# Input product of a second MLP: eight groups of 11 block products per pass become five groups of 15 and one of 6

## The chip, the core and the metric

The program runs on one core of one Trainium2 chip. The metric is the device time of one execution in microseconds. The core has a matrix engine (TensorE, PE in the rows; its weight loads are PEld), VectorE (DVE), ScalarE (ACT), GpSimd (POOL) and SyncE (SP), which here only issues transfers. Each engine runs its own instructions strictly in their written order; they meet at semaphores.

## The reference

```python
x = attn_out.transpose(0, 2, 1, 3).reshape(3072, 384)          # from a linear-attention recurrence
a = x @ w_a;  b = x @ w_b                                      # 384 x 1536 each
x = (a * b) @ w_out                                            # first MLP, 1536 x 384
h = x @ w_in                                                   # second MLP, 384 x 2048: the product that changes
g = np.maximum(h, 0.0) + alpha * np.minimum(h, 0.0)            # alpha: one per column of h
out = g @ w_out2                                               # 2048 x 384
```

All in float32. The kernel takes each factor as a sum of a high and a low part and makes three matmuls (high*high, low*high, high*low) for one product.

## The kernel before, in words

**Stages.** The recurrence and the first MLP share the time up to about 586 us; the second MLP follows. It works transposed: features on the partitions, tokens in the columns. The 3072 tokens are six blocks of 512 and go through in three passes of two blocks (`mlp2(p, ...)`, p = 0, 1, 2). The 2048 hidden features are 16 groups of 128; the 384 inputs are 3 groups of 128, so a product of one feature group with one token block is 3 block products, and a matmul is 128x128 weights by 512 columns.

**Cells.** A cell is two feature groups by two token blocks, 12 block products by the plain rule. The kernel makes 11 (`cell`): sums of weight blocks (`load_c`, `sums` on GpSimd) are multiplied with sums of token blocks (`load_x2`, `comb` on GpSimd, `split` into high and low on ScalarE and VectorE), and the same partial sum serves several results. 11 products by 3 matmuls are 33 matmuls in a cell, 8 cells in a pass. A product or a chain of products runs in one of two PSUM banks (tag `h`, queue `psh`). After a product, a snapshot (`snap`, ScalarE) or an addition into an SBUF tile (`done`, VectorE) takes the bank's value; the bank's next matmul waits for that.

**Activation and output product.** A finished result (`tm`) goes through two Relu instructions on ScalarE, a VectorE instruction with alpha, a high part on ScalarE and a low part on VectorE (`g`). Nine matmuls a result and pass (`outs`) then add it to the six output banks (`oc`), one cell late; they are what TensorE does while a bank of `h` waits. At a pass's end VectorE transposes the six `oc` banks into tiles `O`, and SyncE (in the last pass ScalarE too) writes them out in packets of 128 bytes.

**Weights.** In pass 0 they are made from 64-bit inputs: a load issued by GpSimd, one ScalarE and one VectorE instruction that join the words (`load_w`), then high (ScalarE) and low (VectorE) of every tile; SyncE keeps the tiles in DRAM (`keeps`) and loads them again in passes 1 and 2 (`again`). Tiles live in 37 buffers of tag `w`, which the first MLP's 36 weight tiles hold until their last use.

**The order.** Nothing is ordered by hand. `add` records each step with an engine, an assumed duration, what it reads and writes and the buffer it needs; `Tasks.run` plans all of them with a list schedule, forward and backward eight times, and emits the instructions of the best plan. So every edit can move instructions everywhere.

Of the kernel before, what the change touches and what calls it, by code (L numbers as in the profile page):

```python
# [7 lines left out]
F32 = mybir.dt.float32  # L8
# [11 lines left out]
NT = B * S  # L20
# [347 lines left out]
def rwkv_then_moe_kernel(  # L368
# [721 lines left out]
    SL = {}  # L1090

    def load_x2(p, pr):

        raw, xs = {}, XS[p]
        for n in range(2):
            for kt in range(3):
                s = f"xr{n}{kt}"

                def ld(n=n, kt=kt, s=s):
                    at = 0  # L1100
                    for t, c0, cn in BLOCKS2[2 * p + n]:
# [28 lines left out]
        split("t2", "xr00")  # L1130
        comb("xr11", "xr11", "xr00", ALU.subtract)
        split("t1", "xr11")
        split("b32", "xr12")
        split("b21", "xr01")
        split("b31", "xr02")
        comb("xr01", "xr01", "xr00", ALU.subtract)
        split("t4", "xr01")

    def load_c(e, pr):

        ga = load_w(("i", 2 * e), wt2[2 * e, 0], pr, ["p2"])
        gb = load_w(("i", 2 * e + 1), wt2[2 * e + 1, 0], pr, ["p2"], fin=False)
        next(ga)
        yield
        next(gb)
        yield
        for g in (ga, gb):
# [12 lines left out]
        for i in range(4):  # L1160
            add(*SENG, pr, lambda i=i: sums(i), r=[r0, r1], w=[r1])
        for z, nm in ((1, "ws"), (0, "wc")):
            def hi(z=z, nm=nm):
                W[nm, e] = wp.tile([128, 2, 384], F32R, tag="w", name="w", bufs=NW)
                last = nc.scalar.activation(out=W[nm, e][:, 0], in_=RAW[r1][:, :, z].bitcast(F32), func=ACTF.Copy, scale=256.0).ins
                made["i", 2 * e + 1] = last

            def lo(z=z, nm=nm):
                nc.vector.scalar_tensor_tensor(
                    out=W[nm, e][:, 1], in0=RAW[r1][:, :, z].bitcast(F32), scalar=256.0, in1=W[nm, e][:, 0].bitcast(F32),  # L1170
                    op0=ALU.mult, op1=ALU.subtract)

            add("ACT", 0.455, pr, hi, r=[r1], w=[f"{nm}{e}"] + ([f"wi{2 * e + 1}"] if z == 0 else []), alloc=("w", f"{nm}{e}"))
            add("DVE", 0.46, pr, lo, r=[r1, f"{nm}{e}"], w=[f"{nm}{e}/l"])

    def keeps(e, pr):
        for k, nm in CELL(e, 0):
            add("SP", 0.6, pr, lambda k=k: nc.sync.dma_start(out=wsd[WI[k]], in_=W[k].bitcast(F32).rearrange("p z n -> p (z n)")),
                r=[nm, nm + "/l"], w=[f"kept{nm}"], nbytes=128 * 3072)

    def again(e, p, pr):
        for (k, nm), (k0, nm0) in zip(CELL(e, p), CELL(e, 0)):
            def ld(k=k, k0=k0):
                W[k] = wp.tile([128, 2, 384], F32R, tag="w", name="w", bufs=NW)
                nc.sync.dma_start(out=W[k].bitcast(F32).rearrange("p z n -> p (z n)"), in_=wsd[WI[k0]])

            add("SP", 0.6, pr, ld, r=[f"kept{nm0}"], w=[nm, nm + "/l"], alloc=("w", nm), nbytes=128 * 3072)

    def mlp2(p, pr):

        NE = F2 // 2
        xs, st, acc = XS[p], {}, {}

        def prod(ps, w, k, first, last, more):
            wt, at = w
            n = 0
            for wi, xi in ((0, 0), (1, 0), (0, 1)):
                nc.tensor.matmul(  # L1198
                    out=ps, lhsT=wt[:, wi, at:at + 128], rhs=SL[xs[k][xi]], start=first and n == 0, stop=last and n == 2, skip_group_check=more)
                n += 1  # L1200

        def cell(e, pr):
            par = (NE * p + e) % 2
            b = {}
            (kA, nA), (kB, nB), (kC, nC) = CELL(e, p)[:3]
            WA, WB, WC = (lambda k, x=x: (W[x], 128 * k) for x in (kA, kB, kC))

# [12 lines left out]
            tm = {o: f"TM{o}{par}" for o in range(4)}  # L1220

            def snap(bank, o):
                add("ACT", 0.58, pr - 20, lambda: nc.scalar.copy(SL[tm[o]], b[bank]), r=[f"h{bank}"], w=[tm[o]])  # L1223

            def done(bank, o, f, n):
                x, q, g = tm[o], f"TQ{o % NQ}", f"G{par}{o}"
                s = SL
                add("DVE", 0.69, pr - 20, lambda: tt(s[x], s[x], b[bank], ALU.add), r=[f"h{bank}", x], w=[x])
                if ACTP:
                    add("ACT", 0.62, pr - 20, lambda: nc.scalar.activation(out=s[q], in_=s[x], func=ACTF.Relu, scale=-1.0), r=[x], w=[q])  # L1230
                    add("ACT", 0.62, pr - 20, lambda: nc.scalar.activation(out=s[x], in_=s[x], func=ACTF.Relu), r=[x], w=[x])  # L1231
                    add("DVE", 0.69, pr - 20, lambda: nc.vector.scalar_tensor_tensor(  # L1232
# [329 lines left out]
```

## Time and profile before

| what | before |
|---|---|
| median of 3 runs (lowest, highest) | 979.55 us (977.29, 980.68) |
| the profiled execution | 978.45 us |
| its span, from the first to the last instruction | 976.6 us |
| TensorE busy | 953.7 us, 98% of the span |
| VectorE, ScalarE, GpSimd busy | 739.2, 528.5, 97.2 us |
| mean granted TensorE clock | 0.996 |

The span is 1.85 us shorter than the profiled execution's own time; the rest lies around the first and last instruction. Matmul ends are modelled, and about one matmul record in a hundred is missing, so distances between starts are safer than busy sums.

### The profile page before, as it was taken

The page shows a single profiled execution, that of the slowest core. Times are in us where ns is not written, and L with a number is a line of the kernel's source. Part 1 is how long each engine was busy: PE and PEld are TensorE (multiplying, and loading weights), DVE is VectorE, ACT ScalarE, POOL GpSimd, SP SyncE. Part 2 cuts the span into 40 slices and gives each one's busy share as a digit, 9 for nine tenths or more (in the row PEclk, how much of TensorE's full clock was granted, in tenths as well). Part 3 has the DMA queues.
Part 4 walks back from the last instruction along what each step waited for, and adds up shares of the span by engine and source line. Part 5 has one row for each costly group of instructions (what it writes and reads, how often), then busy time and mean ns, then how long its engine had stood idle before and what let it go on. Part 6 is the DMA issues. An engine that isn't in the chain of part 4 may idle for free.

```text
span 976.6 us, 20832 instructions
## 1 busy us (share of the span) xinstructions
PE 953.7 (98%) x8442; PEld 768.8 (79%) x8442; DVE 739.2 (76%) x1238; ACT 528.5 (54%) x1076; POOL 97.2 (10%) x157
## 2 busy tenths in 40 slices
PE   7999999999999999999999999999999999999996
PEld 4667887788788787888787887888888888888885
DVE  9989999798979998998935566865776455654544
ACT  0657563635444453453443567976766566665652
POOL 1112101000100000010015344110100000000000
PEclk9999999999999999999999999999999999999999
DMA  7797973404153341425025798515357344563203
GB/s 223 192 256 225 252 189 76 134 18 133 51 139 73 109 137 25 133 69 148 7 72 177 254 345 289 178 45 156 104 138 174 115 133 156 149 162 127 65 1 65
DMA packets 141199, 134.15 MB, mean 137 GB/s; under 512 B 101744, under 2 KB 112624, under 8 KB 139824
## 3 DMA queue, kind: packets, MB, share of 16 engines
q1 hardware_dynamic: 127408, 100.59, 36.7%
q0 software_dynamic: 7168, 31.45, 10.1%
q10 hardware_dynamic: 6528, 0.79, 0.5%
q8 instruction: 66, 1.08, 0.5%
q14 instruction: 29, 0.24, 0.1%
HBM read 104.68 MB, written 26.74 MB: 135 GB/s over the span
## 4 chain that ended last, share of the span: by engine, by line
PE 68%; DVE 21%; DMA 5%; issue 3%; ACT 1%; POOL 1%; SPq 0%; ACTq 0%; DVEq 0%; POOLq 0%
PE oc L966 19%; PE acc L966 8%; PE pb L966 8%; PE pa L966 8%; PE hx L1198 6%; PE hy L1198 5%; DVE Tp L414 4%; DVE e L414 4%; DVE A L633 3%; PE hu L1198 3%; PE hv L1198 3%; PE warm L1335 2%; PE psl L714 2%; DVE N L414 2%; DMA raw<-in_wt_dram 2%
## 5 line engine op out<-in xcount | busy, mean ns | idle before, releaser
L966 PE MATMUL acc<-g,w 128*128 128x512 f32 x648 | 173.8, 398 | 0.0
L966 PE MATMUL pb<-x,w 128*128 128x512 f32 x648 | 160.7, 392 | 2.8 <-DVE a L414 2.2
L966 PE MATMUL oc<-gx,w 128*128 128x512 f32 x648 | 162.8, 389 | 0.0
L966 PE MATMUL pa<-x,w 128*128 128x512 f32 x648 | 160.9, 393 | 0.9 <-ACT a L1023 0.9
L966 PEld LDWEIGHTS pb<-x,w 128*128 128x128 f32 x648 | 120.4, 188 | 29.9 <-DVE a L414 3.4
L966 PEld LDWEIGHTS pa<-x,w 128*128 128x128 f32 x648 | 121.2, 188 | 28.2 <-ACT a L1023 2.3
L966 PEld LDWEIGHTS oc<-gx,w 128*128 128x128 f32 x648 | 121.6, 188 | 25.3
L966 PEld LDWEIGHTS acc<-g,w 128*128 128x128 f32 x648 | 119.7, 189 | 24.9
L414 DVE TENSOR_TENSOR Tp<-Tp 112x1024 f32<-112x1024 f32 (+2 forms) x132 | 106.4, 806 | 1.2 <-DMA Tp<-in_rkw_t_dram 0.8
L1032 ACT CAST g<-a 128x512 fp32r<-128x512 f32 x72 | 44.6, 619 | 90.5 <-DVE a L414 74.5
L633 DVE TENSOR_REDUCE A<-e 128x16 f32<-128x768 f32 (+15 forms) x148 | 85.4, 577 | 0.9
L1023 ACT COPY a<-pa 128x512 f32<-128x512 f32 x72 | 42.1, 584 | 79.1 <-PE pa L966 68.0
L1223 ACT COPY tm<-hx 128x512 f32<-128x512 f32 x72 | 42.3, 588 | 77.9 <-PE hx L1198 77.3
L1198 PE MATMUL hx<-xs,w 128*128 128x512 f32 x288 | 80.9, 389 | 0.0
L1232 DVE SCALAR_TENSOR_TENSOR tm<-tm,al 128x512 f32<-128x512 f32 x96 | 72.7, 760 | 5.2 <-ACT tm L1231 5.1
L1230 ACT ACTIVATE tm<-tm 128x512 f32<-128x512 f32 x96 | 60.1, 627 | 24.5 <-DVE tm L414 24.0
L414 DVE TENSOR_TENSOR tm<-tm,hy 128x512 f32<-128x512 f32 x24 | 16.5, 688 | 73.1 <-PE hy L1198 73.1
L414 DVE TENSOR_TENSOR g<-a,g 128x512 fp32r<-128x512 f32 x72 | 49.4, 687 | 27.1 <-ACT g L1032 27.1
L414 DVE TENSOR_TENSOR a<-a,pb 128x512 f32<-128x512 f32 x72 | 48.9, 680 | 27.3 <-PE pb L966 23.0
L1198 PEld LDWEIGHTS hx<-xs,w 128*128 128x128 f32 x288 | 54.1, 188 | 11.3
L1231 ACT ACTIVATE tm<-tm 128x512 f32<-128x512 f32 x96 | 59.9, 625 | 1.4
L453 ACT ACTIVATE ws<-raw 128x384 f16<-128x384 bf16 x68 | 42.8, 642 | 31.3 <-DVE raw L459 15.3
(94 smaller groups left out, 1345.5 us busy)
## 6 DMA issues: line engine op xcount, KB each, us to landing
w<-wsd SPq DMA_DIRECT2D x80, 384.0 KB, 3.1
raw<-in_wt_dram POOLq DMA_DIRECT2D x68, 383.8 KB, 6.2
wsd<-w SPq DMA_DIRECT2D x40, 384.0 KB, 6.4
Tp<-in_rkw_t_dram SPq DMA_DIRECT2D x33, 448.0 KB, 6.1
N<-in_rkw_n_dram SPq DMA_DIRECT2D x10, 1152.0 KB, 5.8
x2d<-x POOLq DMA_DIRECT2D x36, 128.0 KB, 2.3
V<-in_v_s_dram SPq DMA_DIRECT2D x11, 384.0 KB, 4.6
Z<-in_v_s_dram SPq DMA_DIRECT2D x44, 96.0 KB, 3.0
```

What stands on the lines that cost most here:

```text
L414: nc.vector.tensor_tensor(out=out, in0=a, in1=b, op=op)
L453: nc.scalar.activation(out=c["s"].bitcast(F16).rearrange("p (n b) -> p n b", b=2)[:, :, 1], in_=c["raw"].bitcast(BF16)[:, :, 2], func=ACTF ...
L633: nc.vector.tensor_reduce(out=v[:, :, d:d + (n - 1) * (SUB + 1) + 1:SUB + 1], in_=part(st["e"], 0, n), axis=AX.X, op=ALU.add)
L714: nc.tensor.matmul(out=st["ps"][o0:o0 + ms, cc, q, zc * i:zc * i + zc], lhsT=t[b0:b0 + 48, 1, q0 + q, t0:t0 + ms], rhs=r[b0:b0 + 48, q0 + ...
L966: nc.tensor.matmul(out=out, lhsT=lhsT, rhs=rhs, start=start, stop=stop)
L1023: nc.scalar.copy(c["as", f, half][:, cs], c["a", f, half][:, cs])
L1032: nc.scalar.copy(c["g", f][:, 0, cs], c["as", f, half][:, cs])
L1198: nc.tensor.matmul(out=ps, lhsT=wt[:, wi, at:at + 128], rhs=SL[xs[k][xi]], start=first and n == 0, stop=last and n == 2, skip_group_check= ...
L1223: add("ACT", 0.58, pr - 20, lambda: nc.scalar.copy(SL[tm[o]], b[bank]), r=[f"h{bank}"], w=[tm[o]])
L1230: add("ACT", 0.62, pr - 20, lambda: nc.scalar.activation(out=s[q], in_=s[x], func=ACTF.Relu, scale=-1.0), r=[x], w=[q])
L1231: add("ACT", 0.62, pr - 20, lambda: nc.scalar.activation(out=s[x], in_=s[x], func=ACTF.Relu), r=[x], w=[x])
L1232: add("DVE", 0.69, pr - 20, lambda: nc.vector.scalar_tensor_tensor(out=s[x], in0=s[q], scalar=al[:, f:f + 1], in1=s[x], op0=ALU.mult, op1= ...
```

## The change

Cells of three feature groups by two token blocks (18 block products by the plain rule) take 15 products; five of them and one cell with a single feature group (6 products) make a pass. The result of a product is taken from its bank into each result that needs it, with its sign (`TAKES`): the first take of a result is a ScalarE copy, all others are VectorE additions. All products of the 15 use sums of weights in five tiles (two more sums of token blocks, so 15 splits in place of 9). The two token blocks with two runs of rows each, which were the last pair, become the middle pair. The tiles into which x is loaded move to the `w` buffers; there are 9 result tiles in place of 8, and 3 tiles `O` in place of 6 (new ones for the last block).

```diff
-    BLOCKS2 = [[(t, 0, 4)] for t in range(4)] + [[(t, 4, 2), (t + 1, 4, 2)] for t in (0, 2)]
-    XENG, SENG = ("Pool", 1.3), ("Pool", 0.45)
+    BLOCKS2 = [[(0, 0, 4)], [(1, 0, 4)], [(0, 4, 2), (1, 4, 2)], [(2, 4, 2), (3, 4, 2)], [(2, 0, 4)], [(3, 0, 4)]]
+    NQ, NO, NG, NT = 2, 3, 8, 9
+    XENG, SENG, LENG = ("Pool", 1.43), ("Pool", 0.63), ("DVE", 0.55)
+    ORDER = [2, 0, 4, 14, 1, 3, 6, 9, 5, 7, 12, 8, 10, 11, 13]
+    SHORT = [0, 4, 3, 1, 9, 8]
+    CHAIN = {0: 0, 14: 0, 2: 2, 4: 2, 1: 2, 6: 2, 3: 3, 9: 3, 5: 5, 12: 5, 10: 5, 7: 7, 8: 8, 11: 11, 13: 11}
+    TAKES = {0: [(1, -1)], 14: [(5, 1)], 2: [(2, 1)], 4: [(0, 1)], 1: [(1, -1)], 6: [(3, -1)], 3: [(1, 1)], 9: [(0, -1)], 5: [(3, 1)],
+             12: [(2, -1)], 10: [(4, -1), (5, 1)], 7: [(4, 1), (0, -1)], 8: [(0, 1), (5, -1)], 11: [(4, 1)], 13: [(2, 1)]}
...
+        take("w", [raw(k, n) for k in range(3) for n in range(2)] + tmp, make)
...
+                    for n, (wi, xi) in enumerate(((0, 0), (1, 0), (0, 1))):
+                        nc.tensor.matmul(
+                            out=b[ch], lhsT=W[kw][:, wi, 128 * k:128 * k + 128], rhs=SL[x[xi]], start=begin and n == 0, stop=n == 2,
+                            skip_group_check=not begin)
...
+                        if new:
+                            i = nc.scalar.activation(out=SL[x], in_=b[ch], func=ACTF.Copy, scale=float(sign))
+                        else:
+                            i = nc.vector.tensor_tensor(out=SL[x], in0=SL[x], in1=b[ch], op=ALU.add if sign > 0 else ALU.subtract)
+                        for eng, j in reads[ch]:
+                            if eng != new:
...
+                                tc.add_manual_dep(i.ins, j.name, dep, reason="one reader of a bank at a time")
```

TensorE at the end of the first cell of pass 0, before (`hx`, `hy`, `hu`, `hv` are the four chains, `_0` and `_1` the cell; `acc` is the first MLP's output, `oc` the second's):

```order
L966 MATMUL acc_6671<-g_7199,w 128x512 x3
L1198 MATMUL hx_0_7182<-xs,w 128x512 x3
L1198 MATMUL hv_0_7287<-xs,w 128x512 x6
L1198 MATMUL hx_1_7301<-xs,w 128x512 x3
L1198 MATMUL hy_1_7311<-xs,w 128x512 x3
L1198 MATMUL hx_1_7301<-xs,w 128x512 x3
L1198 MATMUL hy_1_7311<-xs,w 128x512 x6
L1198 MATMUL hx_1_7301<-xs,w 128x512 x3
L1198 MATMUL hu_1_7348<-xs,w 128x512 x6
L1198 MATMUL hx_1_7301<-xs,w 128x512 x3
L1198 MATMUL hv_1_7369<-xs,w 128x512 x6
L966 MATMUL oc_7380<-gx,w 128x512 x3
```

The same place in the changed kernel (`h_` with a number is a chain in a bank):

```order
L966 MATMUL acc_6616<-g_7165,w 128x512 x3
L1276 MATMUL h_7158<-xs,w 128x512 x3
L1276 MATMUL h_7216<-xs,w 128x512 x3
L1276 MATMUL h_7239<-xs,w 128x512 x3
L1276 MATMUL h_7247<-xs,w 128x512 x3
L1276 MATMUL h_7239<-xs,w 128x512 x3
L1276 MATMUL h_7269<-xs,w 128x512 x3
L1276 MATMUL h_7239<-gx,w 128x512 x3
L1276 MATMUL h_7287<-gx,w 128x512 x3
L966 MATMUL oc_7295<-gx,w 128x512 x3
```

Between the last `acc` and the first `oc` stood 45 matmuls without others between them, most of two cells; now 24 stand there, all of one cell, in pieces of three.

VectorE in pass 0, before, while TensorE is in the cells that hold `hy_2` and `hu_2` (`tm` takes or alpha steps, `gx` and `gs` low parts, `raw` joins, `w` low parts of weights):

```order
L414 TENSOR_TENSOR tm<-tm,hy_2_7410 128x512
L459 SCALAR_TENSOR_TENSOR raw<-raw,ws_75 128x384
L1243 SCALAR_TENSOR_TENSOR gs<-tm,gs 128x512
L459 SCALAR_TENSOR_TENSOR raw<-raw,ws_76 128x384
L459 SCALAR_TENSOR_TENSOR raw<-raw,ws_77 128x384
L1232 SCALAR_TENSOR_TENSOR tm<-tm,al 128x512
L468 SCALAR_TENSOR_TENSOR w<-raw,w 128x384 x2
L414 TENSOR_TENSOR tm<-tm,hu_2_7527 128x512
```

VectorE in the third cell of pass 0 of the changed kernel (L1294 takes, L1317 alpha, L1320 low parts of `g`, L1221 low parts of summed weights):

```order
L1294 TENSOR_TENSOR tm<-tm,h_7513 128x512
L1317 SCALAR_TENSOR_TENSOR tm<-tm,al 128x512
L459 SCALAR_TENSOR_TENSOR raw<-raw,ws_77 128x384
L1317 SCALAR_TENSOR_TENSOR tm<-tm,al 128x512
L1320 SCALAR_TENSOR_TENSOR gs<-tm,gs 128x512 x2
L1320 SCALAR_TENSOR_TENSOR gx<-tm,gx 128x512 x2
L1294 TENSOR_TENSOR tm<-tm,h_7597 128x512
L1221 SCALAR_TENSOR_TENSOR w<-raw,w 128x384 x2
L1294 TENSOR_TENSOR tm<-tm,h_7617 128x512
L1294 TENSOR_TENSOR tm<-tm,h_7597 128x512
```

Before, the last joins of all weights stand in the third cell; now joins and weight low parts run on through the fourth cell (44 of them behind the first take of pass 0), beside 12 takes a cell.

## Rows read from the trace of the kernel before

**Rows 1.** Windows by stage: us, then busy us (instructions) by engine, clock, DMA share, GB/s

```profile
0.00:586.00 586.00, 571.86 (x6764) 454.37 (x6765) 505.15 (x884) 283.64 (x643) 72.80 (x124) 1.00 0.50 143
586.00:609.00 23.00, 22.31 (x94) 17.11 (x94) 14.75 (x27) 16.22 (x32) 10.43 (x20) 1.00 0.88 306
609.00:640.00 31.00, 31.00 (x139) 25.66 (x138) 26.34 (x43) 27.05 (x52) 5.23 (x8) 1.00 0.46 164
640.00:720.00 80.00, 80.00 (x355) 66.24 (x354) 52.83 (x77) 55.43 (x98) 7.45 (x6) 1.00 0.34 110
968.50:976.60 8.10, 0.01 (x1) 0.00 (x0) 0.77 (x2) 0.00 (x0) 0.00 (x0) 0.75 0.63 103
```

**Rows 2.** Chain that ended last: start, us, engine and line, last stage

```profile
860.40 6.12 PE oc L966 x27
```

**Rows 3.** Timeline of TensorE, end of the first and the second cell

```profile
597.15 1.56 PE L1198 MATMUL hv<-xs,w 128*128 128x512 f32 x6
...
606.46 1.65 PE L1198 MATMUL hv<-xs,w 128*128 128x512 f32 x6
607.96 0.84 PE L966 MATMUL oc<-gx,w 128*128 128x512 f32 x3
```

**Rows 4.** Timeline of VectorE, 631 to 635 us

```profile
631.66 0.55 DVE L1169 SCALAR_TENSOR_TENSOR w<-raw,w 128x384 fp32r<-128x384 f32 x1
632.13 0.68 DVE L414 TENSOR_TENSOR tm<-tm,hv 128x512 f32<-128x512 f32 x1
632.73 0.68 DVE L1243 SCALAR_TENSOR_TENSOR gx<-tm,gx 128x512 fp32r<-128x512 f32 x1
633.33 0.55 DVE L459 SCALAR_TENSOR_TENSOR raw<-raw,ws 128x384 uint32<-128x384 uint32 x1
633.80 0.74 DVE L1232 SCALAR_TENSOR_TENSOR tm<-tm,al 128x512 f32<-128x512 f32 x1
634.46 0.55 DVE L459 SCALAR_TENSOR_TENSOR raw<-raw,ws 128x384 uint32<-128x384 uint32 x1
```

**Rows 5.** Groups by form on GpSimd: count, busy us, mean ns, idle before

```profile
L1158 POOL TENSOR_TENSOR raw<-raw 128x128 f32<-128x128 f32 x32 | 19.4, 625 | 27.8 <-DVE raw L459 27.2
L1123 POOL TENSOR_TENSOR x2r<-x2r 128x512 f32<-128x512 f32 x12 | 17.2, 1436 | 255.8 <-DVE xs L414 186.0 <-DMA x2r<-x2d 69.7
```

**Rows 6.** Timeline of VectorE beside GpSimd sums, three places

```profile
509.67 1.28 DVE L414 TENSOR_TENSOR xs<-x2r,xs 128x512 fp32r<-128x512 f32 x2
511.24 4.83 DVE L414 TENSOR_TENSOR xs<-x2r,xs 128x512 fp32r<-128x512 f32 x3 [0.28 <-ACT xs L1114]
...
625.71 2.42 DVE L468 SCALAR_TENSOR_TENSOR w<-raw,w 128x384 fp32r<-128x384 f32 x2
...
705.32 1.79 DVE L1232 SCALAR_TENSOR_TENSOR tm<-tm,al 128x512 f32<-128x512 f32 x1
```

**Rows 7.** Timeline of GpSimd at the same places

```profile
510.49 5.03 POOL L1123 TENSOR_TENSOR x2r<-x2r 128x512 f32<-128x512 f32 x3 [3.91 <-DVE xs L414]
...
569.67 2.08 POOL L1158 TENSOR_TENSOR raw<-raw 128x128 f32<-128x128 f32 x4 [3.05 <-DVE raw L459]
...
626.70 1.81 POOL L1158 TENSOR_TENSOR raw<-raw 128x128 f32<-128x128 f32 x3
...
704.93 1.62 POOL L1123 TENSOR_TENSOR x2r<-x2r 128x512 f32<-128x512 f32 x1 [5.53 <-DVE xs L414]
```

**Rows 8.** Timeline of the last 17 us: all engines

```profile
961.07 0.72 DVE L1297 STREAM_TRANSPOSE o<-oc 128x512 f32<-128x512 f32 x1 [0.56 <-PE oc L966]
...
963.86 10.62 SPq L1304 DMA_DIRECT2D out_dram<-tm  x20
...
966.31 2.20 PE L966 MATMUL oc<-gs,w 128*128 128x512 f32 x9
```

**Rows 9.** Windows in which tiles O are written: columns as in group 1

```profile
969.00:975.00 6.00, 0.00 (x0) 0.00 (x0) 0.27 (x1) 0.00 (x0) 0.00 (x0) 0.80 0.75 123
725.70:731.70 6.00, 6.00 (x28) 4.96 (x27) 4.45 (x7) 3.18 (x6) 0.00 (x0) 1.00 0.87 163
```

More of the change, by code (lines that the diff above doesn't have):

```diff
@@ L1085, in take @@
+    WI = {k: i for i, k in enumerate(k for e in range(NC2) for k, _ in CELL(e, 0))}
     def take(tag, names, make, parts=("",)):
@@ L1130, in load_x2, with comb @@
[L1130 to L1137, printed above, removed]
-    def load_c(e, pr):
[L1141 to L1147, printed above, removed]
+        def comb(o, a, b, op=ALU.add):
+            add(*XENG, pr, lambda: sums_on(XENG[0], SL[o], SL[a], SL[b], op), r=[a, b], w=[o])
@@ new lines, in load_x2 @@
+        x00, x01, x10, x11, x20, x21 = (raw(k, n) for k in range(3) for n in range(2))
+        comb(tmp[0], x01, x11, ALU.subtract)
+        split(0, tmp[0])
+        comb(tmp[1], x00, x01)
+        split(9, tmp[1])
+        comb(tmp[0], x10, x11)
+        split(14, tmp[0])
+        split(3, x01)
+        comb(tmp[1], x00, x10, ALU.subtract)
+        split(7, tmp[1])
+        comb(x00, x00, x20)
+        split(2, x00)
+        comb(x00, x00, x01)
+        split(4, x00)
+        comb(tmp[0], x01, x10)
@@ new lines, in load_x2 @@
+        split(8, tmp[0])
+        comb(x00, x00, x21)
+        split(1, x00)
+        split(6, x21)
+        comb(x11, x11, x21)
+        split(5, x11)
+        comb(x11, x11, x10)
+        split(12, x11)
+        split(10, x10)
+        comb(x11, x11, x20)
+        split(11, x11)
+        split(13, x20)
+    def load_c(e, pr):
+        n = 3 if e < 5 else 1
+        gs = [load_w(("i", 3 * e + i), wt2[3 * e + i, 0], pr, ["p2"], fin=False) for i in range(n)]
+        for g in gs:
+            next(g)
+            yield
+        for g in gs:
@@ L1160, in load_c @@
[L1160 to L1170, printed above, removed]
+        rs = [f"wi{3 * e + i}r" for i in range(n)]
@@ new lines, in load_c, with hi, lo @@
+        for o, a, b, op in ops:
+            add(*SENG, pr, lambda o=o, a=a, b=b, op=op: sums_on(SENG[0], v(o), v(a), v(b), op), r=rs, w=[rs[o[0]]])
+        for t, i, z, m in tiles:
+            nm = f"wt{e}_{t}"
+            def hi(t=t, i=i, z=z, m=m):
+                W["t", e, t] = wp.tile([128, 2, 384], F32R, tag="w", name="w", bufs=NW)
+                x = nc.scalar.activation(out=W["t", e, t][:, 0, 0:m], in_=RAW[rs[i]][:, 0:m, z].bitcast(F32), func=ACTF.Copy, scale=256.0).ins
+                if z == 0:
+                    made["i", 3 * e + i] = x
+            def lo(t=t, i=i, z=z, m=m):
+                o = W["t", e, t]
+                (nc.gpsimd if LENG[0] == "Pool" else nc.vector).scalar_tensor_tensor(
+                    out=o[:, 1, 0:m], in0=RAW[rs[i]][:, 0:m, z].bitcast(F32), scalar=256.0, in1=o[:, 0, 0:m].bitcast(F32),
@@ L1272, in outs, with out1 @@
+        def outs(e, f, n, pr):
+            if True:
+                g = names[f, n]
+                kw, wo = next(c for c in CELL(e, p) if c[0][:2] == ("p", f))
                 ac = [f"oc{p}{n}_{m}" for m in range(3)]
                 tag, pool = (("acc", "psacc"), ("att", "psatt"))[n]
-                def out1(ks, ms=(0, 1, 2), f=f, g=g, n=n, tag=tag, kw=kw):
+                begin = n not in started
+                started.add(n)
+                end = f == F2 - 1
+                def out1(ks, ms=(0, 1, 2), g=g, n=n, tag=tag, kw=kw, begin=begin, end=end):
@@ L1290, in outs @@
                     add("PE", 3 * MM, pr, lambda out1=out1: out1((2,)), r=[g + "/l", wo], w=ac)
-                if f == F2 - 1:
+                if end:
                     for m in range(3):
                         leave(n, m, pr, ac[m])
+        started = set()
         def leave(n, m, pr, name):
-            o = f"O{(6 * p + 3 * (1 - n) + m) % NO}"
-            add("DVE", 0.69, pr - 20, lambda: nc.vector.transpose(SL[o], acc[n, m]), r=[name], w=[o])
+            k = 6 * p + 3 * (1 - n) + m
+            o = f"O{k % NO}" if p < 2 or k < 12 + NO else f"O{k}"
+            if o not in SL and k >= 12 + NO:
+                add("HOST", 0, 0, lambda: SL.__setitem__(o, wp.tile([128, 512], F32, tag="w", name="o", bufs=NW)), r=["p2"], w=[o], alloc=("w", o))
+            add("DVE", 0.71, pr - 20, lambda: nc.vector.transpose(SL[o], acc[n, m]), r=[name], w=[o])
             def wr(i):
@@ L1484, in rwkv_then_moe_kernel, with make_gh @@
-        for i in range(3):
-            finish(held2, i)
-        take("w", [f"X{i}{z}" for i in range(9, 14) for z in "hl"], make_xh)
+        def make_gh(n):
+            SL[n] = wp.tile([128, 512], F32R, tag="w", name="gs", bufs=NW)
+        for e in range(NC2):
+            q = start[NB - 1] + 4 + 12 * e
+            g = load_c(e, q)
+            n = 3 if e < 5 else 1
+            hs = [load_w(("p", 3 * e + i), wt2[3 * e + i, 1], q + 3, ["p2"]) for i in range(n)]
+            for _ in range(n):
+                next(g)
+            if held2:
+                for h in held2[0]:
+                    for _ in h:
+                        pass
+                keeps(held2[1], held2[2])
+            for h in hs:
+                next(h)
+            for _ in g:
+                pass
+            held2 = hs, e, q
+            if e == 0:
+                take("w", [f"TM{i}" for i in range(7)], make2)
+                take("w", [f"G{i}/{z}" for i in (5, 6, 7) for z in "hl"], make_gh)
@@ L1487, in rwkv_then_moe_kernel @@
+        for h in held2[0]:
+            for _ in h:
+                pass
+        keeps(*held2[1:])
+        take("w", [f"X{i}{z}" for i in range(15, 18) for z in "hl"], make_xh)
         take("w", [f"O{i}" for i in range(1, NO)], make2)
         for p in range(3):
-            load_x2(p, start[NB - 1] if p == 0 else s2 + d * p - 30)
             if p:
-                for e in range(8):
-                    again(e, p, s2 + d * p + d / 8 * e - 20)
-            mlp2(p, lambda e, s=s2 + d * p: s + d / 8 * e)
@@ L1494, in rwkv_then_moe_kernel @@
-        tail.pop()(s2 + 3 * d)
+                load_x2(p, s2 + d * p - 30)
+                for e in range(NC2):
+                    again(e, p, s2 + d * p + d / NC2 * e - 20)
+            mlp2(p, lambda e, s=s2 + d * p: s + d / NC2 * e)
+        for _, f in pend:
+            f(s2 + 3 * d)
         if K.fill:
```

298 lines of the change are left out of this document (140 added, 158 removed).

## Prediction

> **What bounds the kernel now.** I read the windows by stage first [rows 1]. In 609-640 and 640-720 us TensorE is busy for the whole window (31.00 of 31.00, 80.00 of 80.00) at a granted clock of 1.00, its higher level, 2.4 GHz. VectorE has 66% of 640-720 (52.83 us), ScalarE 69%. The chain of waits agrees: after 609 it runs through TensorE, and its link of 27 matmuls in 6.12 us [rows 2] gives the period, 0.2267 us. The second MLP has 8 x 33 x 3 + 864 = 1656 matmuls, 375.4 us at that period; with 21 last ones of the first MLP it is 380.2 of the 382.2 us from 586.3 to 968.5. The one hole is in TensorE's timeline: from 597.15 to 607.96 us [rows 3] 39 matmuls start, worth 8.84 us, so 1.97 us are lost where two cells run without output matmuls between their pieces.
>
> VectorE's timeline gives what one instruction holds the engine for, by the distance of starts in a stretch without gaps [rows 4]: low part of a weight or a join 0.47 us, take or low part of `g` 0.60, alpha step 0.66. (Durations, 0.55 to 0.74, overlap and would count too much.)
>
> The end of the program is a drain: TensorE stops at 968.5, the span ends 8.1 us later with the DMA at 63% [rows 1].
>
> So a matmul less is worth 0.2267 us as long as VectorE keeps pace, and VectorE's load is what grows.
>
> **Matmuls.** A pass had 8 x 11 x 3 = 264 product matmuls and gets (5 x 15 + 6) x 3 = 243; the output product's 864 stay. 63 fewer: -14.28 us. The changed order really holds 729, so this does not depend on the planner. The old hole of 1.97 us goes too; its successor is counted below.
>
> **VectorE and ScalarE.** An old cell had 4 results: 4 additions, 4 alpha steps, 4 low parts, 12 VectorE instructions in 69 matmuls (33 + 36 of output), 15.64 us: 0.77 per us. A new one has 18 takes for 6 results, 12 on VectorE: 24 instructions in 99 matmuls, 22.44 us: 1.07 per us. ScalarE goes from 16 to 24 in the same times, 1.02 to 1.07 per us; from its 69% that is about 72% and costs nothing, hidden under TensorE. In passes 1 and 2 VectorE's 12 takes, 6 alpha, 6 low parts come to 14.8 us of 22.4; some cells add splits or transposes and reach 18.9 of 27.2. VectorE waits there, TensorE doesn't; only the short cell before pass 2 is tight (11.1 us of VectorE work in 6.8), and I put 1 us on it (0 to 2).
>
> **Pass 0** is different. The weights need 77 sums in place of 32 on GpSimd, and a cell's weight tiles and results fill more of the 37 buffers, so fewer cells' weights can be made ahead: joins and low parts of weights now lie between the takes, into the fourth cell. By the changed order VectorE has from the first take to pass 1: 64 takes (38.4), 32 alpha (21.1), 30 low parts (18.0), 17 joins (8.0), 27 low parts of weights (12.7), 12 splits (7.2), 105.4 us; TensorE has 510 matmuls, 115.6 us. Cells two to four stand at 19.1 of 22.4, 22.5 of 23.1, 22.7 of 24.5 us. Without anything else TensorE would stay just ahead.
>
> **GpSimd beside VectorE.** About 47 sums of weights and 11 sums of token blocks fall into pass 0. Alone they take about 0.53 and 1.3 us; the means are 625 and 1436 ns [rows 5], so something holds them up, and VectorE too. Three splits that ran beside three token sums took 4.83 us [rows 6, 7], where 3 x 0.60 + 0.08 = 1.88 is their own: 1.0 us per sum. An alpha step beside one took 1.79 in place of 0.74: 1.05. Two low parts of weights took 2.42 us in place of 1.02 beside three sums of weights and the one before: 0.35 a sum. Yet four sums at 569.67 cost VectorE nothing [rows 7], when it had idle time. Bounds for pass 0: below 8 us (0.08 a sum, 0.4 a token sum, as where VectorE had gaps), above 0.35 x 47 + 1.0 x 11 = 27.5. I take 16, between them, because only part of the instructions will meet a sum: a third are takes, which read a bank, and the take behind the 2.42 us pair ran beside the last sum without loss.
>
> The Trainium skill bears on this ("SBUF — State Buffer", section "Who interferes with whom"): a VectorE instruction with two SBUF inputs and a GpSimd instruction share a port pair and exclude each other for a whole instruction, while a VectorE instruction with one SBUF input is free of it. The rows agree in kind (about 1 us of 1.3 and 0.35 of 0.53 were lost, and the take lost nothing). Taken in full it speaks against the change; what that would cost is the last rival.
>
> VectorE's pass 0 is then 105.4 + 16 = 121.4 us, and with 3% for gaps (my choice; it takes instructions strictly in order and must wait for banks at some) 125.1. Against TensorE's 115.6 that is 9.5 us of stall. It includes the unfilled first cell: 24 product matmuls whose two banks each wait for one or two takes; by hand, with a take at 0.60 to 0.69 us, that alone is 3.4 us, and VectorE works on during it.
>
> **The tail.** The last pair of blocks has one run of rows now, so 24 transfers of 64 KB in place of 48 of 32 KB, the same 1.573 MB. Before, the transposes of the last banks' first half stood early: one at 961.07, and the transfers queue from 963.86, with TensorE's last matmuls from 966.31 [rows 8]. In the changed order the first ones come 4.1 us before TensorE's end. The writes move at 123 GB/s in the tail and 163 in mid-kernel [rows 9], so 9.6 to 12.8 us, begun about 1.2 us before TensorE ends: 8.4 to 11.6 after it, against 8.1. (1.2 is 4.1 less the 2.8 us that lay before from transpose to first transfer.) As half as many issues are needed and these seemed to set the lower rate (DMA at 75%), I take +0.4; bounds -1 and +3. The middle pass now writes with three tiles `O`; the transposes of the next blocks wait for a tile's transfers, but have some 18 VectorE instructions between them, about 12 us, where one tile's share needs 6.5 to 10.5: nothing, with little room.
>
> **Ahead of 586 us** the planner also reorders, and x goes through `w` buffers. TensorE has 14.1 us without work there [rows 1]; I see no term with a sign, and take 0, between -3 and +3.
>
> **Sum.** -14.28 - 1.97 + 9.5 + 1.0 + 0.4 = -5.35 us. The profiled execution's 978.45 (span 976.6 and 1.85 around it) becomes 973.1; the median is 1.1 above it, so 974.2. In general the change is -15.85 us plus S, the stall of TensorE that it brings; it breaks even at S = 15.85.
>
> **Rivals.**
> - *TensorE stays the bound.* Sums meet few two-input instructions, and the loss in pass 0 is that of the first cell and little more, S = 2 to 5. For it: 105.4 is less than 115.6, sums often cost nothing (at 569.67), and VectorE can run ahead of TensorE where weights are concerned. Against: cells three and four have 0.6 and 1.8 us of room for some 20 sums. Time 965.7 to 968.7.
> - *The gain is eaten.* S = 13 to 18, with pass 0 on VectorE and a cost of about 20 to 23 us of the sums: 976.7 to 981.7, not to be told from no change.
> - *VectorE with GpSimd is slower than TensorE was.* Each sum takes its row's loss: 105.4 + 27.5 = 132.9, over 0.97 is 137.0, S = 21.4 + 1: 986. With each sum holding VectorE for its whole time (47 x 0.53 + 11 x 1.3 = 39.2) it is 144.6, S = 29: 993 at most. It decides from 24 us of loss in pass 0. For it: the 2.42 and 4.83 us rows, which are the only ones where VectorE had no slack. Against: takes are free of it, and 569.67. By the rule of the Trainium skill named above ("SBUF — State Buffer"), taken in full, the time is this last one.
>
> That the products are not saved is excluded by the count of 729.
>
> **How the numbers follow.** Full gain 0.27; the forecast (S from 6 to 13, 969.7 to 976.7) 0.42; eaten 0.14; slower 0.17. A measurement of this kernel tells about 0.3%, 2.9 us, from no change. Faster (below 976.6) is the first two less a little: 0.66; same, to 982.5, 0.16; slower 0.18. The range takes the first case's lower end and reaches into the last until about a tenth is left out above: 966 to 985; the likeliest case's own is 969.7 to 976.7.
>
> **What the profile after would show.** Right: about 63 x 0.2267 us less TensorE busy time; in passes 1 and 2 TensorE full, VectorE near 70 to 75%; in pass 0 TensorE waiting some 9 us for takes, `tm` on VectorE named as what ends its waits, VectorE close to 100% busy there, and low parts and alpha steps beside GpSimd sums well over their 0.55 and 0.74 us; the tail 8 to 9 us. Wrong if pass 0 shows only the first cell's 3 us (then 967), if VectorE's instructions there grow to twice their time (then 986 and more), if TensorE waits in passes 1 and 2 as well, which I put at 1 us only, or if the planner lost time ahead of 586 us.

## The result and the profile after

The changed kernel takes 991.9 us (median of 6 runs, 990.25 to 997.51), before 979.74 (6 runs): ratio 1.0136, 95% interval 1.0112 to 1.016. It is slower by 12 us where 5 us of gain were forecast. The profiled execution took 992.5 us, its span 990.7.

Windows by stage, columns as in [rows 1] (us, then busy us and instructions of TensorE, its weight loads, VectorE, ScalarE, GpSimd; clock, DMA share, GB/s):

```profile
0.00:586.00 586.00, 568.79 (x6738) 450.71 (x6739) 504.79 (x865) 275.31 (x623) 80.70 (x126) 0.99 0.46 125
592.00:622.00 30.00, 27.14 (x108) 20.83 (x107) 21.10 (x33) 20.48 (x38) 14.32 (x25) 0.94 0.60 212
622.00:700.00 78.00, 74.44 (x318) 58.69 (x317) 73.31 (x116) 61.04 (x117) 30.66 (x43) 1.00 0.57 200
700.00:760.00 60.00, 56.23 (x240) 44.10 (x239) 57.25 (x81) 41.06 (x74) 18.08 (x11) 1.00 0.67 183
760.00:835.00 75.00, 75.00 (x332) 62.14 (x332) 55.06 (x86) 46.57 (x81) 1.29 (x1) 1.00 0.41 128
835.00:880.00 45.00, 41.29 (x175) 31.66 (x174) 43.65 (x57) 30.12 (x55) 16.45 (x10) 1.00 0.54 156
...
610.70:613.50 2.80, 2.80 (x8) 2.19 (x7) 2.67 (x4) 0.88 (x2) 2.64 (x5) 0.50 0.01 3
```

Where TensorE is full (760 to 835) GpSimd does next to nothing and VectorE has 73%. Where TensorE falls short, GpSimd is at work, and from 622 us on VectorE stands at 94 to 97% there (622 to 700, 700 to 760, 835 to 880). In the first cell (592 to 622) VectorE has only 70%: there TensorE loses time though VectorE isn't full. Before, VectorE had 66% at 640 to 720 and TensorE was full [rows 1].

The account, in the profiled executions. The first product of the second MLP starts at 592.90 us, before at 586.27 (both rows below, before first), with three more matmuls of the first MLP already done (0.68 us): +5.95.

```profile
586.27 0.84 PE L1198 MATMUL hx<-xs,w 128*128 128x512 f32 x3
...
592.90 0.84 PE L1276 MATMUL h<-xs,w 128*128 128x512 f32 x3
```

From there to TensorE's end, 981.97 (the last start and one period), are 1611 matmuls, 365.2 us at 0.2267, in 389.1 us: a stall of 23.9 us; before 1677 matmuls, 380.2 in 382.1: 1.9. The drain, from that end to the end of the span, is 8.75 us, before by the same measure 8.25. So +5.95 + 22.0 - 14.28 + 0.5 = +14.2; the spans differ by 14.1. The 63 matmuls are saved; the stall takes more.

TensorE's timeline (start, us; in brackets the wait and who ended it), first cell and change from pass 1 to 2:

```profile
604.54 0.96 PE L1276 MATMUL h<-xs,w 128*128 128x512 f32 x3 [0.19 <-DVE tm L1294]
605.93 0.96 PE L1276 MATMUL h<-xs,w 128*128 128x512 f32 x3 [0.43 <-DVE tm L1294]
...
609.83 1.10 PE L1276 MATMUL h<-gx,w 128*128 128x512 f32 x3 [2.24 <-DVE tm L1294]
610.73 1.48 PE L966 MATMUL oc<-gx,w 128*128 128x512 f32 x3
612.01 1.48 PE L1276 MATMUL h<-xs,w 128*128 128x512 f32 x3
...
842.04 0.96 PE L1276 MATMUL h<-xs,w 128*128 128x512 f32 x3 [1.14 <-DVE tm L1294]
845.43 0.97 PE L1276 MATMUL h<-xs,w 128*128 128x512 f32 x3 [0.38 <-DVE tm L1294]
848.81 0.96 PE L1276 MATMUL h<-gx,w 128*128 128x512 f32 x3 [1.72 <-DVE tm L1294]
```

TensorE waits for takes (`tm`). Adding what lies between the starts of two rows of this timeline beyond 0.2267 us a matmul, where it exceeds 0.15 us: 5.6 us from 592 to 622, 5.35 to 700, 4.85 to 760, none to 835, 5.1 from 835 to 880; 3.0 more lie in smaller ones. The three matmuls at 610.73 take 1.28 us to the next start in place of 0.68: after the waits up to 2.24 us the granted clock is 0.50 there, its lower level (1.2 GHz), which costs 1.5 us by 613.5.

GpSimd's timeline at two of these places, and its two groups of sums (count, busy us, mean ns), which answer to [rows 5]:

```profile
637.30 12.32 POOL L1103 TENSOR_TENSOR raw<-raw 128x128 f32<-128x128 f32 x15 [7.41 <-DVE raw L459]
...
835.54 4.69 POOL L1103 TENSOR_TENSOR xr<-xr 128x512 f32<-128x512 f32 x3 [2.11 <-PE h L1276]
840.86 6.74 POOL L1103 TENSOR_TENSOR xr<-xr 128x512 f32<-128x512 f32 x4 [0.63 <-DVE gx L1140]
```

```profile
L1103 POOL TENSOR_TENSOR raw<-raw 128x128 f32<-128x128 f32 x77 | 54.1, 722 | 20.7 <-DVE raw L459 18.4
L1103 POOL TENSOR_TENSOR xr<-xr 128x512 f32<-128x512 f32 x33 | 51.9, 1581 | 144.1 <-PE oc L966 98.7 <-DMA xr<-x2d 16.8 <-DVE xs L414 15.6
```

VectorE's timeline beside them:

```profile
641.64 0.67 DVE L1294 TENSOR_TENSOR tm<-tm,h 128x512 f32<-128x512 f32 x1
642.24 1.00 DVE L1317 SCALAR_TENSOR_TENSOR tm<-tm,al 128x512 f32<-128x512 f32 x1
643.16 0.87 DVE L459 SCALAR_TENSOR_TENSOR raw<-raw,ws 128x384 uint32<-128x384 uint32 x1
643.95 0.99 DVE L1317 SCALAR_TENSOR_TENSOR tm<-tm,al 128x512 f32<-128x512 f32 x1
644.87 1.92 DVE L1320 SCALAR_TENSOR_TENSOR gs<-tm,gs 128x512 fp32r<-128x512 f32 x2
...
837.31 1.78 DVE L1317 SCALAR_TENSOR_TENSOR tm<-tm,al 128x512 f32<-128x512 f32 x1
839.01 1.77 DVE L1140 SCALAR_TENSOR_TENSOR gx<-xr,gx 128x512 fp32r<-128x512 f32 x1
840.71 0.68 DVE L414 TENSOR_TENSOR xs<-xr,xs 128x512 fp32r<-128x512 f32 x1
841.31 0.67 DVE L1294 TENSOR_TENSOR tm<-tm,h 128x512 f32<-128x512 f32 x1
```

Beside weight sums an alpha step takes 1.00 us (0.74 in [rows 4]), a join 0.87 (0.55); beside token sums an alpha step 1.78 and a split 1.77. The takes, which read a bank, keep 0.67. In the burst of 15 weight sums nearly every instruction of VectorE with two SBUF inputs is longer by 0.25 to 0.3 us. By the Trainium skill ("SBUF — State Buffer", section "Who interferes with whom") a GpSimd instruction that reads SBUF and a VectorE instruction with two SBUF inputs exclude each other, and a VectorE instruction with at most one SBUF input (a take, whose other input is a PSUM bank) doesn't contend. The rows agree: the takes lose nothing, the others up to 1.04 to 1.1 us of the 1.3 that a token sum takes alone.

### The profile page after: what moved, and what is told of

It reads as the page before. It is cut to its first block, busy times and chain, and to the rows that moved or that the text cites. A ratio compares the mean times of both kernels' runs of the same rounds, so it can differ in the third digit from the quotient of the medians.

```text
span 990.7 us, 21019 instructions
## 1 busy us (share of the span) xinstructions
PE 951.0 (96%) x8379; PEld 757.4 (76%) x8379; DVE 835.0 (84%) x1355; ACT 539.2 (54%) x1097; POOL 166.2 (17%) x223
## 4 chain that ended last, share of the span: by engine, by line
PE 62%; DVE 24%; DMA 5%; issue 4%; ACT 2%; SPq 1%; POOL 1%; DVEq 0%; POOLq 0%; ACTq 0%
PE oc L966 16%; PE h L1276 14%; PE acc L966 10%; PE pb L966 9%; PE pa L966 9%; DVE Tp L414 4%; DVE e L414 3%; DVE A L633 3%; PE psl L714 2%; DVE tm L1294 2%; DMA raw<-in_wt_dram 2%; DVE tm L1317 2%; DVE raw L459 1%; DVE xs L414 1%; DVE N L414 1%
## 5 line engine op out<-in xcount | busy, mean ns | idle before, releaser
L1276 PE MATMUL h<-xs,w 128*128 128x512 f32 x603 | 163.4, 395 | 6.6 <-DVE tm L1294 5.9
L1294 DVE TENSOR_TENSOR tm<-tm,h 128x512 f32<-128x512 f32 x192 | 128.7, 683 | 48.4 <-PE h L1276 43.9
L1276 PEld LDWEIGHTS h<-xs,w 128*128 128x128 f32 x603 | 111.9, 189 | 37.9 <-DVE tm L1294 12.6
L966 PE MATMUL oc<-gs,w 128*128 128x512 f32 x540 | 137.7, 390 | 2.5 <-DVE gs L1320 2.2
L966 PEld LDWEIGHTS oc<-gs,w 128*128 128x128 f32 x540 | 101.1, 188 | 25.1 <-DVE gs L1320 3.6
L1315 ACT ACTIVATE tm<-tm 128x512 f32<-128x512 f32 x96 | 60.3, 628 | 57.7 <-DVE tm L1294 56.2
L966 PE MATMUL oc<-gx,w 128*128 128x512 f32 x324 | 84.6, 393 | 0.0
L1317 DVE SCALAR_TENSOR_TENSOR tm<-tm,al 128x512 f32<-128x512 f32 x96 | 77.4, 814 | 8.3 <-ACT tm L1316 7.8
L1064 POOL DMA_DIRECT2D x2d<-x x36 | 19.3, 541 | 387.3 <-ACT x L1060 387.3
L1292 ACT ACTIVATE tm<-h 128x512 f32<-128x512 f32 x96 | 56.8, 595 | 37.5 <-PE h L1276 32.1
L1103 POOL TENSOR_TENSOR xr<-xr 128x512 f32<-128x512 f32 x33 | 51.9, 1581 | 144.1 <-PE oc L966 98.7
```

The source lines that it names most:

```text
L966: nc.tensor.matmul(out=out, lhsT=lhsT, rhs=rhs, start=start, stop=stop)
L1103: (nc.gpsimd if eng == "Pool" else nc.vector).tensor_tensor(out=out_, in0=a, in1=b, op=op)
L1276: nc.tensor.matmul(out=b[ch], lhsT=W[kw][:, wi, 128 * k:128 * k + 128], rhs=SL[x[xi]], start=begin and n == 0, stop=n == 2, skip_group_che ...
L1292: i = nc.scalar.activation(out=SL[x], in_=b[ch], func=ACTF.Copy, scale=float(sign))
L1294: i = nc.vector.tensor_tensor(out=SL[x], in0=SL[x], in1=b[ch], op=ALU.add if sign > 0 else ALU.subtract)
L1315: add("ACT", 0.626, pr - 20, lambda: nc.scalar.activation(out=s[q], in_=s[x], func=ACTF.Relu, scale=-1.0), r=[x], w=[q])
```

## The experiments

All times are medians, the ratio is to runs of the kernel before on the same chip. "Start" is the first product's start, "stall" as above; both are read from one profiled execution a run.

| run | time, us | ratio (95%) | start | stall |
|---|---|---|---|---|
| before | 979.7 | 1 | 586.3 | 1.9 |
| after | 991.9 | 1.0136 (1.0112, 1.016) | 592.9 | 23.9 |
| a1 small sums | 971.4 | 0.9919 (0.989, 0.9948) | 587.8 | 8.2 |
| c1 small weight sums | 983.9 | 1.0055 (1.0037, 1.0074) | 589.5 | 17.2 |
| c2 small token sums | 977.9 | 0.9977 (0.9961, 0.9993) | 587.5 | 14.7 |
| c3 short alpha | 981.45 | 1.0022 (1.0, 1.0043) | 594.5 | 12.7 |
| a5 small sums, short alpha | 971.8 | 0.9917 (0.99, 0.9933) | 591.4 | 7.5 |
| a2 weight sums on VectorE | 992.1 | 1.0132 (1.01, 1.0164) | 591.25 | 23.5 |
| a4 token sums on VectorE | 990.1 | 1.011 (1.0087, 1.0132) | 590.5 | 24.05 |
| a3 all sums on VectorE | 991.4 | 1.0117 (1.0087, 1.0146) | 588.7 | 21.8 |
| b1 before, new blocks | 976.65 | 0.9972 (0.9956, 0.9989) | 587.0 | 1.85 |
| b2 before, sums twice | 986.8 | 1.0075 (1.0043, 1.0107) | 593.1 | 7.1 |
| b3 b1, weight sums on VectorE | 976.6 | 0.9968 (0.9946, 0.999) | 585.7 | 2.0 |
| b4 b1, all sums on VectorE | 976.0 | 0.9962 (0.9949, 0.9976) | 584.0 | 1.8 |

**a1, small sums.**

```diff
-        (nc.gpsimd if eng == "Pool" else nc.vector).tensor_tensor(out=out_, in0=a, in1=b, op=op)
+        (nc.gpsimd if eng == "Pool" else nc.vector).tensor_tensor(out=out_[:, -8:], in0=a[:, -8:], in1=b[:, -8:], op=op)
...
+            src = raw(0, 1) if s.startswith("xt") else s
...
-                in_=RAW[rs[i]][:, 0:m, z]
+                in_=RAW[rs[i]][:, 0:m, 0]
```

> The changed kernel in the same order of instructions, but every sum of weights and of token blocks on GpSimd covers only 8 columns, and what would read a sum reads a loaded tile of the same size in its place: GpSimd's occupation of the weight and token sums is left out, nothing else. Theory 1 (the sums on GpSimd hold up VectorE's instructions with two SBUF inputs): TensorE's stall after the first product of the second MLP falls from 23.9 us to 4 to 8 us, alpha steps and low parts of pass 0 return to about 0.75 and 0.69 us, time 971 to 977 us. Theory 2 (VectorE's own 1.07 instructions per us, the bank turnaround of two banks): the stall stays above 15 us, time 984 to 991 us. Theory 3 (6.0 us of the loss lie ahead of the second MLP and come from the new order there, not from the sums): the second MLP's first product still begins within 1.5 us of 592.9; by theory 1 in its wide form it begins near 587 to 589.

971.4 us: 20.5 less than after, and the stall at 8.2, just above theory 1's 4 to 8 (the span: 5.1 us ahead, 15.7 in the second MLP). Alpha steps are back at 0.75 us and low parts of `g` at 0.68. Theory 1 holds, theory 2 as a cause by itself falls. The gap of 3.4 us in the first cell that is left is what the prediction had by hand for it. Theory 3 isn't settled by the start: a5, in the same order and with the same cut, starts at 591.4.

**c1 and c2, one kind of sums at a time.** The same cut for the 77 sums of weights (c1), or for the 33 of token blocks (c2, with `== 512`).

```diff
+        if out_.shape[-1] < 512:
+            out_, a, b = out_[:, -8:], a[:, -8:], b[:, -8:]
```

> The changed kernel in the same order; only the 77 sums of weight blocks cover 8 columns (what reads them reads a loaded block in their place), the 33 sums of token blocks are whole. Both kinds small gave the span 20.8 us back: 5.1 ahead of the second MLP and 15.7 in it. If the weight sums are most of it, the stall falls from 23.9 to 14 to 17 us, all of it ahead of 700 us, the 5.1 us at the change from pass 1 to 2 stay, and the time is 976 to 983 us. If the token sums are most of it, the time stays at 985 us or more.

> The changed kernel in the same order; only the 33 sums of token blocks cover 8 columns, the 77 sums of weights are whole. The 5.1 us of stall at the change from pass 1 to 2 fall to about 1 us, those from 700 to 760 us from 4.9 to about 2, and the second MLP begins 2 to 4 us earlier; the stalls from 622 to 700 us stay. Time 980 to 985 us.

c1 gives 8 us, c2 14: together 22, about a1's 20.5. I had expected weight sums to count more: c1 (983.9) lies above its 976 to 983, c2 (977.9) below its 980 to 985. Windows of c2, as above:

```profile
622.00:700.00 78.00, 74.43 (x318) 58.66 (x317) 73.35 (x116) 59.65 (x113) 31.26 (x48) 1.00 0.58 201
700.00:760.00 60.00, 58.70 (x259) 48.00 (x258) 54.58 (x87) 43.52 (x78) 2.22 (x5) 1.00 0.69 190
835.00:880.00 45.00, 44.89 (x196) 36.14 (x195) 37.72 (x60) 27.34 (x50) 2.03 (x3) 1.00 0.71 199
```

and of c1:

```profile
622.00:700.00 78.00, 77.71 (x338) 62.59 (x337) 71.57 (x122) 60.82 (x117) 19.26 (x44) 1.00 0.62 210
700.00:760.00 60.00, 56.20 (x241) 44.31 (x240) 56.91 (x82) 42.10 (x76) 15.03 (x9) 1.00 0.66 178
```

The two parts separate by place: without token sums TensorE is nearly full at the changes of pass (58.70 of 60, 44.89 of 45) and the bursts of weight sums still leave it 3.6 us idle at 622 to 700; without weight sums it is the reverse.

**c3, short alpha steps.**

```diff
-                out=s[x], in0=s[q], scalar=al[:, f:f + 1], in1=s[x], op0=ALU.mult, op1=ALU.subtract)
+                out=s[x][:, -8:], in0=s[q][:, -8:], scalar=al[:, f:f + 1], in1=s[x][:, -8:], op0=ALU.mult, op1=ALU.subtract)
```

> The changed kernel in the same order; the 96 alpha steps on VectorE cover 8 columns of 512, which leaves out the rest of the activation's negative side. All sums and all takes are whole, and nothing between a bank and its next matmul is shorter. Theory A (VectorE's whole load is the limit, its own work and what the sums take from it): some 18 us of VectorE's work leave pass 0 and 3 us each change of pass; the stall falls from 23.9 to 8 to 13 us and the time to 978 to 984 us (the 5 to 6 us ahead of the second MLP stay). Theory B (a take that waits for a sum holds a bank, whatever the load): the stall stays above 18 us, time 987 us or more.

Stall 12.7, 981.45 us: theory A. With all sums whole, taking other work from VectorE gives back 10.5 us, half of what leaving out the sums does. The exclusion is still there: beside a token sum a short alpha step takes up to 1.26 us, where a5, next, has 0.22. So what it costs here depends on VectorE's load: it adds to a VectorE that is full.

**a5, both cuts.**

> The changed kernel in the same order with both cuts at once: all 110 sums cover 8 columns, and so do the 96 alpha steps (the rest of the sums and of the activation's negative side is left out). Small sums alone left a stall of 8.2 us, short alpha steps alone 12.7. If VectorE's load is what is left in both, the stall falls to that of the first cell and a little more, 3 to 5 us, and the time to 965 to 969 us, which is the full gain of the 63 matmuls. If the two banks' turnaround sets the rest, the stall stays at 7 us or more and the time at 970 to 972 us.

971.8 us, stall 7.5: no better than a1. Without the sums VectorE's load is no longer what counts; each wait above 0.15 us that TensorE's timeline still shows ends with a take, and the rest lies in smaller gaps. More than two banks were not tried. So not even a VectorE without these loads would have brought the 967 of the first rival.

**a2, a4, a3: the sums on VectorE.** For a3, and one of the two for a2 and a4:

```diff
-    XENG, SENG, LENG = ("Pool", 1.43), ("Pool", 0.63), ("DVE", 0.55)
+    XENG, SENG, LENG = ("DVE", 0.69), ("DVE", 0.25), ("DVE", 0.55)
```

> The changed kernel with its 77 sums of weight blocks on VectorE in place of GpSimd (the sums of token blocks stay), planned anew. Theory 1: the sums cost VectorE some 0.25 us each, 47 x 0.25 = 12 us in pass 0, but nothing is held up by them any more; the bursts of GpSimd in pass 0 with 0.99 us alpha steps are gone, pass 0 stalls 5 to 10 us less, time 981 to 988 us. Theory 2 (VectorE's load decides): 12 us more load on VectorE make it slower, 992 to 1002 us.

> The changed kernel with its 33 sums of token blocks on VectorE (0.60 us each) and the weight sums left on GpSimd, planned anew. Leaving the token sums out gave 14 us. If what costs is that a GpSimd sum holds VectorE up for its own 1.0 to 1.1 us, 33 x 0.4 us are saved: part of 13 us, so 980 to 987 us. If VectorE's work at the two changes of pass is too much anyway, as with all sums on VectorE: 989 to 993 us.

> The changed kernel with all sums, weights and token blocks, on VectorE, planned anew. Theory 1: also the stall of 5.1 us at the change from pass 1 to 2 and of 3 to 5 us at that from pass 0 to 1 shrink, since a sum of token blocks costs VectorE 0.6 us in place of about 1.0 by contention: 976 to 986 us. Theory 2: 990 to 1005 us.

None moves the time by more than 2 us: 992.1, 990.1, 991.4, all in the range of the theory by which VectorE's work decides. In a3 no sum on GpSimd holds VectorE up, but it does them itself (groups of a3 on VectorE, 592 to 976 us: count, busy us, mean ns):

```profile
L1103 DVE TENSOR_TENSOR xr<-xr 128x512 f32<-128x512 f32 x22 | 14.8, 682 | 0.7 <-PE h L1276 0.7
...
L1103 DVE TENSOR_TENSOR raw<-raw 128x128 f32<-128x128 f32 x47 | 13.1, 285 | 0.1
```

28 us of its time in place of what the exclusion took. Theory 1's gain from moving the sums was wrong: on either engine they cost VectorE about as much. Added up over the whole run, VectorE's instructions take 921.3 us in after, 882.3 in a1 and 925.1 in a3 (planned anew): 39.0 us more beside GpSimd's sums, 42.8 more with the sums on VectorE.

**b1, before with the new blocks alone.** 
```diff
-    BLOCKS2 = [[(t, 0, 4)] for t in range(4)] + [[(t, 4, 2), (t + 1, 4, 2)] for t in (0, 2)]
+    BLOCKS2 = [[(0, 0, 4)], [(1, 0, 4)], [(0, 4, 2), (1, 4, 2)], [(2, 4, 2), (3, 4, 2)], [(2, 0, 4)], [(3, 0, 4)]]
```

> The kernel before with only the new arrangement of token blocks (those of two row runs in the middle pair). The tail: 24 writes of 64 KB in place of 48 of 32 KB; 8.1 us after TensorE's end becomes 7 to 9. Theory 3 (the plan ahead of the second MLP moves by some us with any edit): the first product of the second MLP begins elsewhere than 586.3, by up to 6 us; otherwise within 1 us. Time 976 to 983 us.

976.65 us, 0.3% less than before; the drain is 7.5 us in place of 8.25, the start 0.7 us later. So this edit doesn't move the start by several us, as theory 3 has it of any. The other part of the 2 us isn't located: the profiled spans, 976.5 and 976.6, don't show it.

**b2, before with each weight sum done twice.**

```diff
-            (nc.gpsimd if SENG[0] == "Pool" else nc.vector).tensor_tensor(out=o, in0=a, in1=b, op=op)
+            for _ in range(2):
+                (nc.gpsimd if SENG[0] == "Pool" else nc.vector).tensor_tensor(out=o, in0=a, in1=b, op=op)
```

> The kernel before in its order, each of its 32 sums of weights on GpSimd done twice (64; the changed kernel has 77). Theory A: VectorE has slack there and takes the loss; the time moves by at most 3 us, 977 to 982. Theory B: each further sum costs what one of the changed kernel's costs, 32 x 0.2 to 0.3 us: 985 to 989 us.

986.8 us, the number of theory B, but at the place where TensorE waits longest VectorE isn't slowed by a sum: it waits for one. GpSimd, VectorE and TensorE, each by its timeline:

```profile
590.32 5.82 POOL L1159 TENSOR_TENSOR raw<-raw 128x128 f32<-128x128 f32 x8 [3.23 <-DVE raw L459]
```

```profile
595.21 0.56 DVE L1170 SCALAR_TENSOR_TENSOR w<-raw,w 128x384 fp32r<-128x384 f32 x1 [2.06 <-ACT w L1166]
596.75 0.56 DVE L1170 SCALAR_TENSOR_TENSOR w<-raw,w 128x384 fp32r<-128x384 f32 x1 [0.98 <-ACT w L1166]
597.22 0.68 DVE L414 TENSOR_TENSOR a<-a,pb 128x512 f32<-128x512 f32 x1
```

```profile
597.96 0.97 PE L1199 MATMUL hy<-xs,w 128*128 128x512 f32 x3 [3.38 <-DVE a L414]
```

The sums end at 596.1; up to 596.75 VectorE waits twice, idle, for a weight's high part, and the step `a` that TensorE needs stands behind these in its order. So a sum can have a second price: lateness, in an order that was planned for a shorter one. This place holds 3.4 of the 5.2 us by which the stall grew. The profiled execution is the slowest of the five (990.3 us), so its late start (593.1) isn't read as a price of the sums.

**b3 and b4: the old scheme, new blocks, sums on VectorE.** On b1, for b4 (b3 moves the second pair alone):

```diff
-    XENG, SENG = ("Pool", 1.3), ("Pool", 0.45)
+    XENG, SENG = ("DVE", 0.69), ("DVE", 0.25)
```

> The scheme of before (11 products) with the new arrangement of token blocks, which alone gave 976.7 us (0.997 of before), and its 32 sums of weights on VectorE in place of GpSimd, planned anew. Doubling them on GpSimd cost 7 us, so a sum there costs some 0.2 us even where VectorE has slack, through the time in which the weights become ready and VectorE's next instruction waits for them. If lateness is the cost, 0.2 us on VectorE in place of 0.53 to 0.63 in series on GpSimd brings 1 to 4 us: 973 to 976. If VectorE's time is the cost, no change: 976 to 978.

> As the run before this one, and the 12 sums of token blocks on VectorE too. Their cost before: two of them lie at changes of pass where TensorE never waited, so nothing more is expected than 0 to 1 us: 972 to 977.

976.6 and 976.0 us: as b1, within the intervals. By the terms set for b3 that speaks against lateness as a price of the 32 sums where they are planned for; b2 shows it only for sums that the plan didn't know of. b4 beats both kernels (0.9962); what it shares with b1, the arrangement of blocks, brings most of it.

## Why the prediction was wrong

The step that failed is the stall put down to the sums: it was worked out for pass 0 alone and there as an average (+9.5 us), with nothing for sums at the changes of pass (+1.0 without them) and nothing ahead of the second MLP. Measured are 14.3 us in pass 0, 6.6 at the changes of pass, 3.0 in small gaps and 5.95 ahead, of which the sums are only a part. The mechanism, TensorE waiting for takes of a VectorE that GpSimd's sums slow down, was right; waits in passes 1 and 2 and lost time ahead of the second MLP stood among its signs of being wrong.

The time is that of the last rival (VectorE with GpSimd slower than TensorE was, 986 to 993 us, at the chance of 0.17), but its number agrees by luck: it has 27.5 to 39.2 us of VectorE's time lost to sums in pass 0, where some 14 are measured. Its upper end also leaves out the 3% for gaps that its lower end has; with them, and the 1 us, it would be 998. By the prediction's steps:

- **Matmuls, -14.28 us**: right; the account above closes with it. TensorE's busy time, which was to show it, fell by 2.7 us only (953.7 to 951.0): the modelled end of a matmul lies 0.16 us behind the next one's start (0.84 us for three that take 0.68), so part of every wait counts as busy. **Passes 1 and 2 full where no sums run**: right (760 to 835). **Tail +0.4**: measured +0.5. **First cell 3.4 us**: right without weight sums (a1, c1), 5.6 with them and the lower clock. (Before, 42 matmuls stood there without others between them, not 45.)
- **Where the sums were priced**: "About 47 sums of weights and 11 sums of token blocks fall into pass 0" is right, but 30 sums of weights and 22 of token blocks run elsewhere. The section on the change speaks of two more sums of token blocks; it is 11 a pass in place of 4. Pass 2's eleven fall at the change from pass 1 to 2, where 1 us was put and 5.1 measured (0.8 in c2); pass 0's own stand ahead of the second MLP. c2 gives 14 us for the 33.
- **The change from pass 0 to 1**, where nothing was put, has one wait of 1.5 us (744.04) that a1, c1, c2, c3 and a5 keep in the same size, so neither the sums nor the alpha steps make it: the take that TensorE needs (743.34) stands behind a transpose of an `oc` bank (742.71) in VectorE's order.
- **The price of a sum** was about right: alpha steps, low parts, joins and splits of 592 to 727 us are together some 14 us longer than in a1 (by the means, 30 alpha steps by 0.17, 20 joins by 0.12, 28 low parts by 0.14, 8 splits by 0.34); 16 were taken, between bounds of which no row shows the lower one's 0.08 and 0.4 us. **Its conversion into stall** was not: 9.5 us by averaging VectorE's work over pass 0, measured 14.3. The sums come in bursts of 15 (12.3 us) in which VectorE falls behind and two banks don't cover it; at other times in pass 0 it waits 8 us for banks. The 3% for gaps was a choice without a row.
- **Ahead of the second MLP, 0 +- 3**: measured +5.95. From the recurrence's last matmul group to the first product are 80.2 us, 77.5 in a1, c2 and a5: the token sums hold TensorE up by 2.7 us there. The kernel before, with 496 matmuls on that way in place of 460, loses 1.6 us there too (87.3 us; 85.7 in b3 and b4, with the weight sums on VectorE), so 1.0 us of the 5.95 is shown. The other 4.9 lie ahead of that group (512.7 us in place of 499.0, with 39 matmuls more done) and stay open: it starts at 510.0 to 514.3 us in the six profiles of this same order, a spread nearly as large. The three that start it last (after, c3, a5) have two dips of the granted clock to 0.50 before it, a1 one, c1 and c2 none; before has one.

The misses add up: 4.8 in pass 0, 5.6 at the changes of pass, 3.0 in small gaps, 6.0 ahead: 19.4 us from 973.1 to 992.5. The rule of the Trainium skill on the shared port pair ("SBUF — State Buffer", as above) had been kept as a rival; the rows then at hand held few places where VectorE had no slack, and those showed the full price.

## What to carry to other kernels

Count every instance of a side job over the whole program and note beside which stretch each runs, before pricing those in one stretch: 22 of 33 token sums and 30 of 77 weight sums were outside the stretch that was summed. An engine that is near full in a stretch should be costed by its worst burst against the number of banks or buffers that cover it, not by the mean. A GpSimd sum with SBUF operands isn't free help for VectorE: here it cost VectorE about what doing it itself would have cost, and a scheme that trades matmuls for such sums and takes pays only while VectorE has room.

## What was unexpected of the hardware

A token sum of 1.3 us made a VectorE instruction with two SBUF inputs beside it up to 1.04 to 1.1 us longer, yet takes not at all (0.67 us). Cut to 8 columns, the sums on GpSimd still took 313 and 368 ns by the profile, but cost VectorE nearly nothing (alpha steps 0.75 us in a1). TensorE's granted clock fell to 0.50 after waits of 0.19, 0.43 and 2.24 us (604 to 610); after 0.35 and 1.95 us (a1) it stayed at 1.00.
